# Two first-layer activations put behind the first query copies on ScalarE, and one turned tile copied by ScalarE in place of VectorE

## The chip, the core and the metric

The kernel runs on one core of one Trainium2 chip. The core has a matrix engine (TensorE, "PE" in the profile, with its weight loads listed apart as "PEld"), VectorE ("DVE"), ScalarE ("ACT"), GpSimd ("POOL") and SyncE ("SP"), which here only issues transfers. Each engine works through its own list of instructions in order, and the lists meet through semaphores. The metric is the device time of one execution in microseconds. Three runs of the kernel before gave 180.80, 180.94 and 180.96 us, so the median is 180.94 us.

## The reference

One input x of 2048 rows by 512 is layer-normalised to xn, and two branches are added to x:

```
xn = layernorm(x)
out = x + A(xn) + B(xn)

A: q, k, v = xn @ wqkv, in 32 heads of 16
   pq = q @ w_phi (per head); pk = k @ w_phi
   phi = concat(softmax(p), softmax(-p))        # 32 features per head
   kv  = sum over rows of phi_k^T v;  z = sum over rows of phi_k
   o   = (phi_q @ kv) / (phi_q . z + 1e-6);  A = o @ wo

B: act = mish(xn @ w1 + b1)                     # 512 -> 1792
   B   = act @ w2                               # 1792 -> 512
```

The attention is linear: the sums over all 2048 keys must be complete before the first query can be finished. Branch B needs no such sum, and its matrix products can be put wherever TensorE would otherwise be waiting.

## The kernel before

The 2048 rows are 16 tiles of 128 rows, in four groups of four. The order of every engine's list is the order in which the Python code issues its instructions; no scheduler changes it. The kernel keeps x, the turned xn (`xnT`), and the first layer's results (`acts`) in SBUF for the whole run.

**The head (lines 510 to 537).** The first four row tiles are normalised one by one. Each normalised tile is turned by four 128x128 transposes on TensorE into a PSUM bank (`ln_turn_pe`, line 151), and one copy takes the bank to `xnT` (line 157). The caller names the engine of this copy: tile 0 goes through ScalarE (`act`), tiles 1, 2 and 3 through VectorE (`dve`). `logits(0, i)` (line 205) multiplies turned tile i by the folded key weights `wkp` and has ScalarE copy the result to `p_sb`. On TensorE the order is: second half of the product for tile 1, transposes of tile 3 (line 532), a small transpose of the bias (line 534), products of tile 2, products of tile 3 (line 537), then the value products of the first four tiles, then six units of the first layer (`hidden(6)`, line 553), then the key products of row tile 4 (line 564).

**The key stages (lines 555 to 599).** For each group of four tiles VectorE takes maxima and minima over the 16 features (`extremes`), ScalarE the exponentials, VectorE the sums and the division (`normalise`). TensorE meanwhile does the key and value products, the accumulation of the key sums and units of the first layer. A unit (`hidden`, line 185) is one of 56: four matmuls into a bank `ph`, then one Mish activation on ScalarE (line 198), which frees the bank. Fifty-four of the 56 units are issued by line 598.

**The query stages (lines 604 to 694).** The last key stage is followed by queries in pairs of row tiles. The exponentials of a row tile go through a transposing DMA (`turn`, line 254, tile `qT`). `attend(h, i)` (line 330) handles row tile i of pair h: 32 small matmuls multiply the turned features by the masked key sums into the four banks `pnd`, then two ScalarE copies empty these banks, denominators to `ds` (line 353), numerators to `wkp` or `wv`, which are used as scratch by then (line 359). There is one `pnd` buffer, so the matmuls of an `attend` wait until both copies of the `attend` before it are done. `combine` (line 363) divides on VectorE and sends the result through a transposing DMA. `second_layer(t, f0, f1)` (line 411) adds products f0 to f1 of the 14 second-layer products of row tile t to a bank `po`. `project_out` adds the output projection to the same bank and `residual` adds x.

In this part the ordinary banks come from one pool of four, `ps`. When the first `attend` is issued they hold `po` of row tile 0, the two `ph` banks of the last two first-layer units, and `po` of row tile 1. `po` of row tile 2 therefore takes the bank of the first of the two units, and `po` of row tile 3 that of the second. The two units belong to the last group of rows; their results are read from row tile 12 on.

The lines around the second edit are 613 to 619:

```
second_layer(0)
hidden(2)
attend(0, 0)
second_layer(1, 0, 12)
attend(0, 1)
extremes(5, halves=low)
second_layer(1, 12)
```

Of the kernel before, what the change touches and what calls it, by code (L numbers as in the profile page):

```python
# [12 lines left out]
ACT = mybir.ActivationFunctionType  # L13
# [5 lines left out]
def kernel(  # L19
# [12 lines left out]
    nc = tc.nc  # L32
# [33 lines left out]
    def bank(name, dtype=FP32, pool=None):  # L66
        pool = pool or next(turns[0])
        return pool.tile([P, 512], dtype, name=name, tag="mm")

    def three_banks(name, bufs):  # L70
        stack = ExitStack()
        return stack, stack.enter_context(tc.tile_pool(name=name, bufs=bufs, space=PSUM))
# [3 lines left out]
    acts = persist.tile([P, FT, S], BF16, name="acts")  # L76
# [7 lines left out]
    b1f = wts.tile([P, FT], FP32, name="b1f")  # L84
# [66 lines left out]
    def ln_turn_pe(t, xn, i, copy):  # L151
        ptr = bank("ptr", BF16)
        for kt in range(KT):
            nc.tensor.transpose(
                ptr[:, kt * P : (kt + 1) * P], xn[:, i, kt * P : (kt + 1) * P], ident[:]
            )
        copy(xnT[:, t, :, :], ptr[:].rearrange("p (k c) -> p k c", k=KT))
# [7 lines left out]
    def project(w, t, pp=None, kts=range(KT)):  # L165

        if pp is None:
            pp = bank("pproj")[:]
        for kt in kts:
            nc.tensor.matmul(  # L170
                pp, lhsT=xnT[:, t, kt, :], rhs=w[:, kt, :],
                start=(kt == 0), stop=(kt == KT - 1),
            )
        return pp
# [7 lines left out]

    units = iter([(g, f) for g in range(NG) for f in range(FT)])

    def hidden(n, pool=None):

        for _ in range(n):
            g, f = next(units)
            ph = bank("ph", FP32, pool)
            for kt in range(KT):  # L190
                nc.tensor.matmul(  # L191
                    ph[:],
                    lhsT=w1_sb[:, kt, f * P : (f + 1) * P],
                    rhs=xnT[:, g * TPG : (g + 1) * TPG, kt, :],
                    start=(kt == 0),
                    stop=(kt == KT - 1),
                )
            nc.scalar.activation(  # L198
                acts[:, f, g * 512 : (g + 1) * 512], ph[:], ACT.Mish, bias=b1f[:, f : f + 1]
            )  # L200


    p_of, e_of, qT_of = {}, {}, {}
# [9 lines left out]
    def extremes(s, between=None, halves=(slice(0, TPG),)):  # L213

        if s not in e_of:
            e_of[s] = epool.tile([P, TPG, 2, 512], BF16, name="e")
        for q in halves:
            n = q.stop - q.start
            e = e_of[s][:, q]
            pv = p_of[s][:, q, :].rearrange("p t (c e) -> p (t c) e", e=16)  # L220
            for pl, op in enumerate((ALU.max, ALU.min)):
                if pl == 1 and between is not None:
                    between()
                src = pv
                for half in (8, 4, 2):
                    m = smx.tile([P, 128, half], BF16, name=f"m{half}", bufs=1)[:, 0 : n * 32, :]
                    nc.vector.tensor_tensor(  # L227
                        out=m, in0=src[:, :, 0:half], in1=src[:, :, half : 2 * half], op=op
                    )
                    src = m  # L230

                m = smx.tile([P, 128, 1, 2], BF16, name="m1", bufs=1)[:, 0 : n * 32]
                nc.vector.tensor_tensor(out=m[:, :, 0, :], in0=src, in1=src[:, :, ::-1], op=op)
                mb = m.rearrange("p (t c) u o -> p t c u o", t=n).to_broadcast([P, n, 32, 8, 2])
                p5 = pv.rearrange("p (t c) (e o) -> p t c e o", t=n, o=2)
                nc.vector.tensor_tensor(  # L236
                    out=e[:, :, pl, :].rearrange("p t (c e o) -> p t c e o", e=8, o=2),
                    in0=p5 if pl == 0 else mb,
                    in1=mb if pl == 0 else p5,
                    op=ALU.subtract,  # L240
                )
# [88 lines left out]
    def attend(h, i):  # L330

        if i == 0:
            nd_of[h] = (
                (wkp, wv)[h % 2][:].rearrange("p (i l) c -> p i l c", i=2),
                opool.tile([P, 2, 2, 64], FP32, name="ds"),
            )
        nm, ds = nd_of[h]
        pnd = later[0].tile([P, 4, 512], FP32, name="pnd", tag="nd")
        for pl in range(2):
            for j in range(4):  # L340
                for r in range(4):
                    at, rows = (pl * 4 + j) * 36, slice(32 * r, 32 * r + 32)
                    nc.tensor.matmul(  # L343
                        pnd[:, r, at : at + 36],
                        lhsT=qT_of[h][rows, i, pl * 4 + j, :],
                        rhs=kvm[rows, pl, j, :],
                        start=True,
                        stop=True,
                        tile_position=(32 * r, 0),
                    )  # L350
        a = pnd[:, :, 0:288].rearrange("p r (l j c) -> p l j r c", l=2, j=4)
        to = nm[:, i, :, :].rearrange("p l (j r c) -> p l j r c", j=4, r=4)
        nc.scalar.copy(  # L353
            ds[:, i].rearrange("p x (g r h) -> p g r x h", g=8, r=4),
            pnd[:, :, 0:288].rearrange("p r (g c) -> p g r c", g=8)[:, :, :, 32:36].rearrange(
                "p g r (x h) -> p g r x h", x=2
            ),
        )
        nc.scalar.copy(to, a[:, :, :, :, 0:32])
# [45 lines left out]
    def halves(t):  # L405
        return (slice(0, 256), slice(256, 512)) if t == NT - 1 else (slice(0, 512),)

    def second_layer(t, f0=0, f1=FT):
        if f0 == 0:
            po_of[t] = [  # L410
                bank("po", FP32, later[1] if c.stop == 512 and c.start else None)
                for c in halves(t)
            ]
        for po, c in zip(po_of[t], halves(t)):
            for f in range(f0, f1):
                nc.tensor.matmul(  # L416
                    po[:, c], lhsT=acts[:, f, t * P : (t + 1) * P], rhs=w2_sb[:, f, c],
                    start=(f == 0), stop=False,
                )
# [55 lines left out]
    dve, act = nc.vector.tensor_copy, nc.scalar.copy  # L475
# [10 lines left out]
    xn = lnp.tile([P, TPG, D], BF16, name="xn", tag="xn")  # L486
# [42 lines left out]
    p1 = project(wkp, 1, kts=range(0, 2))  # L529
    ln_turn_pe(2, xn, 2, dve)  # L530
    act(p_of[0][:, 1, :], project(wkp, 1, p1, kts=range(2, 4)))
    ln_turn_pe(3, xn, 3, dve)
    pb = bank("pb", BF16)
    nc.tensor.transpose(pb[:, 0:FT], b1b[:], ident[0:FT, 0:FT])
    nc.vector.tensor_copy(b1f[:], pb[:, 0:FT])
# [11 lines left out]
    xn = lnp.tile([P, TPG, D], BF16, name="xn", tag="xn")  # L547
# [3 lines left out]
    for i in range(TPG):  # L551
        value(i, act)
    hidden(6)

    for s in range(NG):
# [6 lines left out]
        if s == 0:  # L562
# [3 lines left out]
            stack, pool = three_banks("pw", 1)  # L566
# [10 lines left out]
        if ln:  # L577
            t0 = (s + 2) * TPG
            st = ln_stats(t0, TPG)
            xn = lnp.tile([P, TPG, D], BF16, name="xn", tag="xn")  # L580
# [8 lines left out]
        if s == 0:  # L589
            hidden(6)  # L590
            act(p_of[1][:, 1:4, :], wide[:])
            wide = None
            stack.close()
            pk = upper.enter_context(tc.tile_pool(name="pk", bufs=1, space=PSUM))
            pz = upper.enter_context(tc.tile_pool(name="pz", bufs=2, space=PSUM))
            hidden(6)
            turns[0] = cycle([pz, ps, ps, pz, ps, px, ps])
# [13 lines left out]
    turns[0] = cycle([ps])  # L611
    later = [after.enter_context(tc.tile_pool(name="pq", bufs=1, space=PSUM))]
    second_layer(0)
    hidden(2)
    attend(0, 0)
    second_layer(1, 0, 12)
    attend(0, 1)
    extremes(5, halves=low)
    second_layer(1, 12)
    combine(0, first)  # L620
    combine(0, last)
    extremes(5, halves=high)
# [102 lines left out]
```

## Time and profile before

The profile is of one execution of 180.87 us, 0.07 us under the median of the three runs. Its span, from the first to the last instruction, is 178.7 us; 2.1 us lie around it.

| what | value |
|---|---|
| execution profiled | 180.87 us |
| span | 178.7 us |
| TensorE clock granted | 0.999 |
| PE busy | 171.6 us, 96% of the span |
| DVE busy | 153.7 us, 86% |
| ACT busy | 124.0 us, 69% |
| ScalarE table loads for the first layer, each | 1.28 us |
| ScalarE copy of a 128x512 bank to SBUF | 0.59 us |
| VectorE copy of a turned 128x512 tile | 0.41 to 0.42 us |

All times inside the profile are counted from the start of the span. Busy shares say little on what a given edit is worth; the chain of waits and the timeline of the stage that is edited say more. Ends of matmuls are modelled in the records, so short gaps on PE are best read from the starts of successive matmuls.

### The profile page before, as it was taken

How to read it: one execution, taken by the hardware profiler on the slowest of the kernel's cores; microseconds unless marked ns; L12 is line 12 of the kernel's file. 1: busy time of each engine (PE TensorE's matmuls, PEld its weight loads, DVE VectorE, ACT ScalarE, POOL GpSimd, SP SyncE). 2: the span in 40 equal slices, each digit the busy share in tenths (PEclk: the TensorE clock that was granted, in tenths of full speed). 3: DMA queues.
4: the chain of work that ended last, by engine and by line, in shares of the span. 5: the costliest groups of instructions: out<-in, count | busy, mean ns of one | idle time of the engine just before them, and what ended most of it. 6: DMA issues, size and time to landing. Idle time of an engine off the chain costs nothing.

```text
span 178.7 us, 4338 instructions
## 1 busy us (share of the span) xinstructions
PE 171.6 (96%) x1806; PEld 81.7 (46%) x1806; DVE 153.7 (86%) x305; ACT 124.0 (69%) x166; POOL 28.5 (16%) x40
## 2 busy tenths in 40 slices
PE   6799999999999999999999989999999999999992
PEld 2454444454444545544454444444444444444561
DVE  1989799999999989998999969798789979789853
ACT  3657999997998799969994988388223854552200
POOL 5203029900799300000000000000000000000000
PEclk9999999999999999999999999999999999999999
DMA  5997794330023600000000883919983096394843
GB/s 143 292 417 271 137 366 144 59 64 0 4 53 64 121 0 0 4 4 0 0 4 0 159 80 71 110 31 146 201 126 90 0 150 118 88 122 120 67 115 115
DMA packets 44559, 18.12 MB, mean 101 GB/s; under 512 B 36988, under 2 KB 44028, under 8 KB 44540
## 3 DMA queue, kind: packets, MB, share of 16 engines
q1 hardware_dynamic: 43712, 17.57, 46.8%
q10 hardware_dynamic: 828, 0.28, 0.6%
q8 instruction: 14, 0.23, 0.6%
q14 instruction: 5, 0.04, 0.1%
HBM read 6.84 MB, written 2.10 MB: 50 GB/s over the span
## 4 chain that ended last, share of the span: by engine, by line
DVE 46%; PE 42%; ACT 5%; DMA 4%; issue 2%; DVEq 0%; ACTq 0%
PE po L416 21%; DVE s L268 10%; PE pproj L170 8%; PE po L425 6%; DVE m L227 6%; DVE e L281 6%; DVE e L236 6%; DVE r L276 4%; PE ph L191 3%; DVE stats L130 3%; ACT e L249 2%; PE pnd L343 2%; DMA qT<-e 2%; DMA x_sb<-in_A_x_dram 2%; DVE r L277 2%
## 5 line engine op out<-in xcount | busy, mean ns | idle before, releaser
L416 PE MATMUL po<-w_sb,acts 128*128 128x512 bf16 (+1 forms) x238 | 51.0, 367 | 0.2 <-DVE x_sb L433 0.2
L191 PE MATMUL ph<-xnT,w_sb 128*128 128x512 bf16 x224 | 49.5, 379 | 0.0
L249 ACT ACTIVATE e<-e 128x2048 bf16<-128x2048 bf16 (+1 forms) x17 | 30.2, 1808 | 7.8 <-DVE e L236 7.8
L198 ACT ACTIVATE acts<-ph,b1f 128x512 bf16<-128x512 f32 x56 | 34.4, 706 | 1.5 <-PE ph L191 1.4
L191 PEld LDWEIGHTS <-w_sb 128*128 128x128 bf16 x224 | 21.9, 98 | 26.4 <-issue 0.3
L416 PEld LDWEIGHTS <-acts 128*128 128x128 bf16 x238 | 22.2, 98 | 22.7 <-issue 0.2
L170 PEld LDWEIGHTS <-xnT 128*128 128x128 bf16 x192 | 18.3, 98 | 21.8 <-issue 1.1
L268 DVE TENSOR_REDUCE s<-e 128x128 f32<-128x2048 bf16 x8 | 18.2, 2273 | 1.6 <-ACT e L249 1.6
L353 ACT COPY ds<-pnd 128x128 f32<-128x128 f32 x16 | 4.4, 275 | 17.7 <-PE pnd L343 15.5
L142 POOL TENSOR_SCALAR xn<-x_sb,mv,rstd 128x512 bf16<-128x512 bf16 x8 | 16.6, 2084 | 0.2
L433 DVE TENSOR_TENSOR x_sb<-po,x_sb 128x512 bf16<-128x512 f32 (+1 forms) x17 | 10.9, 658 | 6.6 <-PE po L425 6.5
L425 PE MATMUL po<-wqk,ob 128*128 128x512 bf16 (+1 forms) x68 | 15.1, 367 | 0.0
L170 PE MATMUL pproj<-wv,xnT 128*128 128x512 bf16 x64 | 15.0, 379 | 0.0
L227 DVE TENSOR_TENSOR m<-m 128x256 bf16<-128x256 bf16 (+2 forms) x44 | 13.4, 304 | 1.5
L170 PE MATMUL pproj<-wqk,xnT 128*128 128x512 bf16 x64 | 14.5, 379 | 0.0
L211 ACT CAST p_sb<-pproj 128x512 bf16<-128x512 f32 x20 | 10.8, 587 | 3.8 <-PE pproj L170 2.3
L170 PE MATMUL pproj<-wkp,xnT 128*128 128x512 bf16 x52 | 12.6, 379 | 0.1
L281 DVE TENSOR_TENSOR e<-e,r 128x2048 bf16<-128x2048 bf16 x8 | 10.7, 1337 | 0.3
L227 DVE TENSOR_TENSOR m<-p_sb 128x1024 bf16<-128x1024 bf16 (+1 forms) x18 | 10.2, 565 | 0.0
L425 PEld LDWEIGHTS <-ob 128*128 128x128 bf16 x68 | 6.4, 97 | 7.0 <-DMA ob<-ob 0.4
L236 DVE TENSOR_TENSOR e<-p_sb,m 128x2048 bf16<-128x2048 bf16 (+1 forms) x9 | 8.9, 989 | 0.3
L236 DVE TENSOR_TENSOR e<-m,p_sb 128x2048 bf16<-128x2048 bf16 (+1 forms) x9 | 8.9, 989 | 0.3
(73 smaller groups left out, 173.7 us busy)
## 6 DMA issues: line engine op xcount, KB each, us to landing
w_sb<-in_B_w_dram SPq DMA_DIRECT2D x2, 1792.0 KB, 8.4
out_dram<-x_sb SPq DMA_DIRECT2D x15, 128.0 KB, 1.9
x_sb<-in_A_x_dram SPq DMA_DIRECT2D x1, 1024.0 KB, 11.0
x_sb<-in_A_x_dram SPq DMA_DIRECT2D x1, 512.0 KB, 4.1
wv<-in_A_wqkv_dram SPq DMA_DIRECT2D x1, 512.0 KB, 4.8
wqk<-in_A_wo_dram SPq DMA_DIRECT2D x1, 512.0 KB
x_sb<-in_A_x_dram SPq DMA_DIRECT2D x1, 256.0 KB, 3.1
x_sb<-in_A_x_dram ACTq DMA_DIRECT2D x1, 256.0 KB, 3.5
```

What stands on the lines that cost most here:

```text
L142: engine.tensor_scalar(out=xn[:, at + i, :], in0=x_sb[:, t0 + i, :], scalar1=mv[:, i, 0:1], scalar2=rstd[:, i : i + 1], op0=ALU.subtract, ...
L170: nc.tensor.matmul(pp, lhsT=xnT[:, t, kt, :], rhs=w[:, kt, :], start=(kt == 0), stop=(kt == KT - 1),)
L191: nc.tensor.matmul(ph[:], lhsT=w1_sb[:, kt, f * P : (f + 1) * P], rhs=xnT[:, g * TPG : (g + 1) * TPG, kt, :], start=(kt == 0), stop=(kt == ...
L198: nc.scalar.activation(acts[:, f, g * 512 : (g + 1) * 512], ph[:], ACT.Mish, bias=b1f[:, f : f + 1])
L227: nc.vector.tensor_tensor(out=m, in0=src[:, :, 0:half], in1=src[:, :, half : 2 * half], op=op)
L236: nc.vector.tensor_tensor(out=e[:, :, pl, :].rearrange("p t (c e o) -> p t c e o", e=8, o=2), in0=p5 if pl == 0 else mb, in1=mb if pl == 0 ...
L249: nc.scalar.activation(v, v, ACT.Exp)
L268: nc.vector.reduce_sum(t[:], v.rearrange("p t l (c e) -> p (t l c) e", e=16), axis=AX.X)
L281: nc.vector.tensor_tensor(out=vv, in0=vv, in1=r2[:, :, None, :].to_broadcast([P, 128, 8, 2]), op=ALU.mult)
L416: nc.tensor.matmul(po[:, c], lhsT=acts[:, f, t * P : (t + 1) * P], rhs=w2_sb[:, f, c], start=(f == 0), stop=False,)
L425: nc.tensor.matmul(po[:, c], lhsT=oT_of[h][:, t % 2 * 4 + j, :], rhs=wo_sb[:, j, c], start=False, stop=(j == 3),)
L433: nc.vector.tensor_tensor(out=y, in0=po[:, c], in1=y, op=ALU.add)
```

## The change

There are two edits.

The copy of the fourth turned tile (tile 3) goes from VectorE to ScalarE. On ScalarE it stands between the copies of the logits of tile 1 and tile 2. VectorE's list is one instruction shorter, ScalarE's one longer.

The last two units of the first layer keep their matmuls where they were, but their two Mish activations are held back and issued after `attend(0, 0)`. On ScalarE the two copies of `attend(0, 0)` then come first, followed by the table load for Mish, the two activations, and the copies of `attend(0, 1)`. Two of the second-layer products of row tile 1 move from ahead of `attend(0, 1)` to behind it, so there are ten ahead and four behind. The number of table loads stays the same, since copies ask for none.

```diff
-    def hidden(n, pool=None):
+    def hidden(n, pool=None, late=None):
...
-            nc.scalar.activation(
-                acts[:, f, g * 512 : (g + 1) * 512], ph[:], ACT.Mish, bias=b1f[:, f : f + 1]
-            )
+            if late is None:
+                activate(g, f, ph)
+            else:
+                late.append((g, f, ph))
+
+    def activate(g, f, ph):
+        nc.scalar.activation(
+            acts[:, f, g * 512 : (g + 1) * 512], ph[:], ACT.Mish, bias=b1f[:, f : f + 1]
+        )
...
-    ln_turn_pe(3, xn, 3, dve)
+    ln_turn_pe(3, xn, 3, act)
...
     second_layer(0)
-    hidden(2)
+    late = []
+    hidden(2, late=late)
     attend(0, 0)
-    second_layer(1, 0, 12)
+    for unit in late:
+        activate(*unit)
+    second_layer(1, 0, 10)
     attend(0, 1)
     extremes(5, halves=low)
-    second_layer(1, 12)
+    second_layer(1, 10)
```

## The prediction

> **What bounds the kernel now.** I read the page first, then the chain of waits in order of time, then the timelines of the two places that the change edits, 9.5 to 13.8 us and 100 to 113 us. The page gives two engines that are nearly full, and a chain that is shared between them:
>
> ```profile
> span 178.7 us, 4338 instructions
> PE 171.6 (96%) x1806; PEld 81.7 (46%) x1806; DVE 153.7 (86%) x305; ACT 124.0 (69%) x166; POOL 28.5 (16%) x40
> DVE 46%; PE 42%; ACT 5%; DMA 4%; issue 2%; DVEq 0%; ACTq 0%
> ```
>
> The chain in order of time (start, length, what) tells which engine holds which stretch:
>
> ```profile
> 10.76 5.29 PE pproj L170 x24
> 16.04 5.18 PE ph L191 x24
> 21.22 0.88 PE pproj L170 x4
> 22.12 0.69 DVE p_sb L564
> ...
> 98.00 3.19 DMA qT<-e
> 101.24 0.46 PE pnd L343 x32
> ...
> 104.89 0.38 PE pnd L343 x32
> 105.27 3.56 PE po L416 x16
> ```
>
> From about 8 to 22 us PE holds the path, without a gap; from 22 to 98 VectorE does; from 101 to 155 PE again; VectorE from 155 to 165 and PE to the end. The reader should see that the first edit lies in a PE stretch although it lightens VectorE, and that the second lies where PE takes over. There PE has one real gap, and the timeline names its cause:
>
> ```profile
> 101.21 1.28 ACT L198 ACT_TABLE_LOAD   x1
> 102.51 1.27 ACT L198 ACTIVATE acts<-ph,b1f 128x512 bf16<-128x512 f32 x2
> 103.66 0.27 ACT L353 COPY ds<-pnd 128x128 f32<-128x128 f32 x1
> 103.81 1.03 ACT L359 CAST wkp<-pnd 128x1024 bf16<-128x1024 f32 x1
> 104.89 0.38 PE L343 MATMUL pnd<-kvm,qT 32*128 32x36 bf16 x32 [0.59 <-ACT wkp L359]
> 105.37 0.28 ACT L353 COPY ds<-pnd 128x128 f32<-128x128 f32 x1 [0.53 <-PE pnd L343]
> ```
>
> The first query's matmuls are done at about 101.7, but ScalarE first loads a table and runs two activations, so the copies that free `pnd` end at 104.84 and the second query starts at 104.89. For the head:
>
> ```profile
> 10.46 0.59 ACT L531 CAST p_sb<-pproj 128x512 bf16<-128x512 f32 x1 [0.50 <-PE pproj L170]
> 10.68 0.42 DVE L157 COPY xnT<-ptr 128x512 bf16<-128x512 bf16 x1 [0.23 <-PE ptr L154]
> 11.76 0.59 ACT L211 CAST p_sb<-pproj 128x512 bf16<-128x512 f32 x1 [0.72 <-PE pproj L170]
> 22.12 0.69 DVE L564 CAST p_sb<-pproj 128x512 bf16<-128x512 f32 x1 [1.06 <-PE pproj L170]
> ```
>
> **First edit, the fourth turned tile.** VectorE loses one copy of 0.42 us. The bias copy of 0.16 us behind it still has to wait for its own transpose, whose record ends at 10.76, so VectorE is ahead by about 0.25 us, not 0.42. That is worth nothing: at 22.12 VectorE stands idle for 1.06 us for a PE product, and PE's stretch up to there is gapless, so it waits 1.3 us instead. What covers it is PE's 11 us of products from 10.76 on.
>
> ScalarE gains a copy of 0.59 us (tile 0's copy, same shape, is 0.59 at 6.64). It stands in a hole: 0.72 us of idle time before the cast at 11.76. Two casts back to back take 1.07 us from 7.17 on, so a second starts 0.48 us after the first; the new copy would start at 10.46 + 0.48 = 10.94 and end at 11.53. The cast at 11.76 is not delayed. But PE needs this tile: products of tile 2 run at one per 0.216 us from 10.69, so tile 3's first is due at 11.56, and its weight load stood at 11.35. From an engine's end to PE's start the rows show 0.05 us (ScalarE ends 104.84, PE starts 104.89), so the weights can be loaded from 11.58 on. The stall is at least 0.02 us, if the matmul may follow its load at once, as at 10.69 where both are recorded together; at most 0.22, if the copy waits for the full end of the cast at 11.05 (end 11.64, plus 0.05) and a whole weight load of 0.10 is exposed. I take 0.07, nearer the overlapping start, since the rows at 7.17 show ScalarE starting early. PE has no gap between here and 22.1, nor VectorE from there to 98 (it only waits for exponentials that it fed itself), so this stall goes to the end in full: +0.07.
>
> **Second edit, the order around the first query.** TensorE's matmuls are the same in number. From one `attend` to the next the rows give 3.44 us with 14 products between (108.76 to 112.20) and 3.87 with 16 (104.89 to 108.76): 0.215 per product and 0.43 fixed. Without a wait the second query would have started at 101.24 + 0.43 + 12 x 0.215 = 104.25; it started at 104.89. The wait is 0.64 us (the timeline says 0.59, from a modelled end).
>
> In the changed order ScalarE is free at 101.20 and takes the first query's copies when its matmuls are done. At the second query the copy starts 0.48 us after the matmuls (105.37 against 104.89), so here at 101.72, or 0.04 later for the wait on two semaphores in its queue: 101.76. The numerators' copy follows 0.17 later and frees `pnd` at 102.95. TensorE comes to the second query after ten products, at 101.24 + 0.43 + 2.15 = 103.82, 0.87 us later than that. Its turned features landed at 102.61 by the trace's landing events, so they don't hold it. Two products fewer ahead means two more behind, and the third query starts at 103.82 + 0.43 + 18 x 0.215 = 108.12 instead of 108.76: -0.64. If only the record's gap of 0.59 counts, -0.59.
>
> What is queued behind the copies: table load 102.96 to 104.24, activations 104.25 to 105.52, the second query's denominators at about 105.39. Before, these stood at 105.37. So ScalarE is no later for anything behind, its idle 0.53 us has only moved ahead of the first copies; its exponential stays at 107.87. The activations themselves are late by 1.75 us. Their results are not read for 40 us, but their banks are: `po` of row tile 2 takes the first one's bank, a wait that the changed program carries on that first matmul. PE comes there at 103.82 + 0.31 + 4 x 0.215 = 104.99; the first activation ends 0.69 after its start, at 104.94, plus 0.05 is 104.99. That is a dead heat: between 0 and, if every step on ScalarE slips a little, 0.12. I take 0.02.
>
> One rule speaks against this order. The rows show a table load beginning within 0.02 us of the end of the work before it (101.21 after 101.19; 106.57 after 106.56) and the next activation 0.01 to 0.02 after it. The Trainium skill, "ScalarE: Activation LUTs", section "What ACT_TABLE_LOAD costs", adds a drain of about 1.38 us to each load of 1.283; by it the first activation would end near 106.3 and the sum would be slower by some 0.8 us instead. The trace agrees on the load's 1.28 and shows no drain in any of its other loads, so the sum goes by the rows.
>
> VectorE can combine the first row tile from 102.93 instead of 103.97, the second when its denominators come at 105.66, with the numerators at 106.56 on time: about 0.6 us earlier than before, and SP issues the two transposing DMAs behind it earlier (106.42 and 108.74 before). No queue is passed: SP's order is unchanged. PE needs their result at about 111.9; it landed at 111.36 even before.
>
> Does the 0.64 last? The next claim on ScalarE's own pace is `pnd` for the fourth query: ScalarE is busy with exponentials until 109.78, its copies end at 110.85, PE now comes at 111.56: 0.7 us to spare. By 112.68 ScalarE waits 1.83 us for PE, by 113.58 VectorE waits 1.04 us, so from there everything is paced by PE and moves with it, the VectorE stretch from 155 included, whose start waits on a PE product (0.90 us idle at 155.03).
>
> **Sum.** -0.64 + 0.02 + 0.07 = -0.55 us against the profiled execution of 180.87 us, which is 180.32. That execution is 0.07 under the median of 180.94; a median of the changed kernel may lie as much above the sum.
>
> **Rivals.**
> 1. Forecast: about 180.3, faster by 0.3%. Chance 0.73, own range 180.1 to 180.5.
> 2. The gain shrinks below about what a measurement of this kernel can tell from no change (0.2%, 0.36 us): tile 3's stall at its upper 0.22 and the bank wait at 0.12, with the gain at 0.59, gives -0.25, so 180.6. For it: both waits are close races. Against: each would have to come out at its worst end. Chance 0.12.
> 3. The gain is hidden: PE runs 0.64 earlier into another wait that doesn't move, ScalarE's copies for the fourth query or the DMA for the projection. Then only the head's stall is left: 180.87 + 0.07 = 180.9. Against: 0.7 and over 1 us to spare. Chance 0.06.
> 4. Slower: the first `ph` bank comes late. If the changed place of the table load costs ScalarE as much again as one load, 1.28 us, row tile 2's first product waits 1.28 us at 104.99, and -0.64 + 1.28 + 0.07 + 0.02 gives 181.6. It decides from 0.6 us of lateness on. Against: no load in the rows costs more than 1.3 us with its edges. The drain that the Trainium skill states in the section named above would do this. Chance 0.09, with other ways to be slower in it.
>
> The predicted time is that of case 1. The range 180.05 to 180.75 holds cases 1 and 2 with a run's scatter (0.16 us over the three runs). Faster by over 0.2%: 0.73; within 0.2%: 0.18; slower: 0.09.
>
> **What would show it.** Right: on ScalarE denominators at about 101.8, the table load at about 103; no wait of PE on `wkp` before the second query, which starts near 103.9; the third query near 108.2; PE's idle time down by about 0.5 us; VectorE's wait at 22 us grown to 1.3. Wrong: a wait of PE on `acts` before row tile 2, a weight load of tile 3 waiting on ScalarE for more than 0.2 us, or the fourth query waiting on `wv`.

## The result, and the profile after

The changed kernel takes 180.30 us (median of eight runs) against 180.88 us for the kernel before in the same session. One of the eight, the profiled one, ran at a granted TensorE clock of 0.76, took 225.76 us and is left out of everything that follows. The other seven lie between 180.09 and 180.57, with a mean of 180.28 and a median of 180.19. Their ratio to the kernel before is 0.9967, with a 95% interval of 0.9956 to 0.9978: faster by 0.60 us, between 0.40 and 0.80. The forecast was 180.32 us. All lines of "after" below are of a second session of the same kernel, whose profiled execution took 180.09 us with the clock at 1.000. There the ratio is 0.9949, interval 0.9936 to 0.9961.

In the changed kernel's file, lines behind `hidden` have moved down by six: 343 is 349, 353 is 359, 359 is 365, 416 is 422, 425 is 431, 433 is 439 and 564 is 570.

The page after, first lines and the chain by engine:

```profile
span 178.0 us, 4338 instructions
PE 171.9 (97%) x1806; PEld 81.6 (46%) x1806; DVE 153.4 (86%) x304; ACT 124.5 (70%) x167; POOL 28.5 (16%) x40
...
PE 87%; DVE 8%; DMA 2%; issue 0%; DVEq 0%
```

VectorE has one instruction less, ScalarE one more, TensorE is at 97%. The chain is now followed back along TensorE for nearly the whole span. That does not mean that VectorE has become fast: in this execution TensorE reached the first query just as its data did (the data landed at 101.29 us, the matmuls start at 101.33), so at that point the inferred chain could turn either way. In the profile of the second edit alone, where the first query starts at the same 101.33, the page gives VectorE 45% and TensorE 43%.

The place of the second edit, in the timeline after (ScalarE, then TensorE):

```profile
100.72 0.56 ACT L217 CAST p_sb<-pproj 128x512 bf16<-128x512 f32 x1
101.86 0.27 ACT L359 COPY ds<-pnd 128x128 f32<-128x128 f32 x1 [0.58 <-ACT p_sb L217]
102.02 1.02 ACT L365 CAST wkp<-pnd 128x1024 bf16<-128x1024 f32 x1
103.06 1.28 ACT L204 ACT_TABLE_LOAD   x1
104.35 1.26 ACT L204 ACTIVATE acts<-ph,b1f 128x512 bf16<-128x512 f32 x2
105.51 0.27 ACT L359 COPY ds<-pnd 128x128 f32<-128x128 f32 x1
```

```profile
101.33 0.37 PE L349 MATMUL pnd<-kvm,qT 32*128 32x36 bf16 x32
101.64 2.33 PE L422 MATMUL po<-w_sb,acts 128*128 128x512 bf16 x10
103.90 0.37 PE L349 MATMUL pnd<-kvm,qT 32*128 32x36 bf16 x32
104.21 4.06 PE L422 MATMUL po<-w_sb,acts 128*128 128x512 bf16 x18
108.20 0.37 PE L349 MATMUL pnd<-kvm,qT 32*128 32x36 bf16 x32
```

The copies of the first query come first and free `pnd` at 103.04; TensorE comes at 103.90 and does not wait. The wait of 0.59 us on `wkp` is gone. From the first query to the third it now takes 6.87 us (101.33 to 108.20); before it was 7.52 (101.24 to 108.76), as this line of the kernel before shows with the ones of the prediction:

```profile
108.76 0.37 PE L343 MATMUL pnd<-kvm,qT 32*128 32x36 bf16 x32
```

That is 0.65 us gained, and the eighteen products run on across the bank that the late activation frees. The single starts show how close that was: the first product of row tile 2 starts at 105.090, 0.050 us after the first activation ends (105.040) and 0.222 us after the product before it, where the usual distance is 0.216. So TensorE lost 0.006 us there.

The head (ScalarE, TensorE's weight loads, VectorE):

```profile
10.54 0.58 ACT L537 CAST p_sb<-pproj 128x512 bf16<-128x512 f32 x1 [0.50 <-PE pproj L170]
11.02 0.59 ACT L157 COPY xnT<-ptr 128x512 bf16<-128x512 bf16 x1
...
11.66 0.98 PEld L170 LDWEIGHTS <-xnT 128*128 128x128 bf16 x6 [0.35 <-ACT xnT L157]
...
22.24 0.69 DVE L570 CAST p_sb<-pproj 128x512 bf16<-128x512 f32 x1 [1.32 <-PE pproj L170]
```

TensorE's weight loads pause for 0.35 us before tile 3's. Counted from the first product of tile 2, tile 3's first weight load comes 0.90 us later, before 0.66, so it is 0.24 us late. In the kernel before it stood 0.214 us, a whole matmul, ahead of the product that uses it, and that covers most of the delay: from the first product of tile 2 to the first value product the starts are 1.773 us apart, before 1.737. The stall is 0.04 us. VectorE waits 1.32 us for the key product instead of 1.06.

0.65 less 0.04 is 0.61, yet the span is 0.75 us shorter, although this execution's first rows of x landed about 0.1 us later (VectorE's first statistics start at 4.05, before at 3.95) and its first query started 0.10 us later. At the third query it is 0.56 us ahead of the kernel before, at SyncE's last instruction named DRAIN 0.57, at the end of the span 0.75. So about 0.2 us came from somewhere that the sum did not have, and it came at the very end. The experiments were aimed at that, and at the two close races.

### The profile page after: what moved, and what is told of

It reads as the page before. It is cut to its first block, busy times and chain, and to the rows that moved or that the text cites. A ratio compares the mean times of both kernels' runs of the same rounds, so it can differ in the third digit from the quotient of the medians.

```text
span 223.7 us, 4338 instructions
## 1 busy us (share of the span) xinstructions
PE 219.0 (98%) x1806; PEld 92.5 (41%) x1806; DVE 154.7 (69%) x304; ACT 129.0 (58%) x167; POOL 28.7 (13%) x40
## 4 chain that ended last, share of the span: by engine, by line
PE 95%; DMA 3%; SPq 0%; DVE 0%; issue 0%
PE po L422 29%; PE ph L191 28%; PE pproj L170 23%; PE po L431 8%; DMA wT<-in_A_wqkv_dram 3%; PE pnd L349 2%; PE pkv L302 2%; PE pwide L170 2%; PE pfold L112 1%; PE ptr L154 0%; SPq L449 0%; DVE x_sb L439 0%; PE pb L540 0%
## 5 line engine op out<-in xcount | busy, mean ns | idle before, releaser
L422 PE MATMUL po<-w_sb,acts 128*128 128x512 bf16 (+1 forms) x238 | 65.4, 442 | 0.0
L191 PE MATMUL ph<-xnT,w_sb 128*128 128x512 bf16 x224 | 64.7, 462 | 0.0
L204 ACT ACTIVATE acts<-ph,b1f 128x512 bf16<-128x512 f32 x56 | 37.5, 687 | 16.5 <-PE ph L191 16.4
L191 PEld LDWEIGHTS <-w_sb 128*128 128x128 bf16 x224 | 25.1, 112 | 38.0 <-issue 38.0
L422 PEld LDWEIGHTS <-acts 128*128 128x128 bf16 x238 | 25.4, 112 | 31.9 <-issue 29.3
L431 PE MATMUL po<-wqk,ob 128*128 128x512 bf16 (+1 forms) x68 | 19.3, 443 | 0.0
L170 PE MATMUL pproj<-wv,xnT 128*128 128x512 bf16 x64 | 19.2, 458 | 0.0
L170 PE MATMUL pproj<-wqk,xnT 128*128 128x512 bf16 x64 | 18.8, 462 | 0.0
L170 PE MATMUL pproj<-wkp,xnT 128*128 128x512 bf16 x52 | 15.8, 459 | 0.0
L178 DVE CAST vext<-pproj 128x512 bf16<-128x512 f32 x6 | 4.1, 691 | 14.3 <-PE pproj L170 14.3
```

The lines of the kernel that those rows point to most:

```text
L170: nc.tensor.matmul(pp, lhsT=xnT[:, t, kt, :], rhs=w[:, kt, :], start=(kt == 0), stop=(kt == KT - 1),)
L191: nc.tensor.matmul(ph[:], lhsT=w1_sb[:, kt, f * P : (f + 1) * P], rhs=xnT[:, g * TPG : (g + 1) * TPG, kt, :], start=(kt == 0), stop=(kt == ...
L204: nc.scalar.activation(acts[:, f, g * 512 : (g + 1) * 512], ph[:], ACT.Mish, bias=b1f[:, f : f + 1])
L422: nc.tensor.matmul(po[:, c], lhsT=acts[:, f, t * P : (t + 1) * P], rhs=w2_sb[:, f, c], start=(f == 0), stop=False,)
L431: nc.tensor.matmul(po[:, c], lhsT=oT_of[h][:, t % 2 * 4 + j, :], rhs=wo_sb[:, j, c], start=False, stop=(j == 3),)
```

## The experiments

Every time below is compared with runs of the kernel before in the same session; ratios have 95% intervals, and the microseconds are the ratio's difference from 1 times the median of before.

### Both edits again, and each alone

First the changed kernel itself, from which the lines above come.

> Both edits, nothing else, for an undisturbed profile. Theory (the gap at the second query closed, a small stall in the head, a dead heat at row tile 2's bank): -0.55 us against the kernel before; denominators' copy at about 101.8, table load about 103.0, second query about 103.9, third about 108.2; weight load of tile 3 waits on ScalarE 0.02 to 0.2 us. Rival (the bank comes late): PE waits on acts before row tile 2's first product by 0.1 us or more. Rival (the gain is hidden behind a later wait): third query 0.6 us earlier, but PE's start on the row tiles after 113 us no earlier than before.

Measured: 0.9949 (0.9936 to 0.9961), 180.11 us against 181.07. The events came within 0.1 us of the forecast's marks (101.86, 103.06, 103.90, 108.20). There is no wait on `acts` in its list of waits, and the starts above put the bank's share at 0.006 us, so the bank is not late by anything that counts. The shift is not hidden either: the first matmul behind the fourth query's projection, at 114.32 us before, starts at 113.76, and from the fifth query to SyncE's last drain it takes 60.22 us in the changed kernel and 60.23 before.

Then the first edit alone (the edit is against the changed kernel, as the next one is):

```diff
-    hidden(2, late=late)
+    hidden(2)
...
-    second_layer(1, 0, 10)
+    second_layer(1, 0, 12)
...
-    second_layer(1, 10)
+    second_layer(1, 12)
```

> The first edit alone: tile 3 copied by ScalarE, the order around the first query as before. Theory: +0.07 us against the kernel before (0.02 to 0.22), PE's weight load of tile 3 waits on ScalarE, VectorE's wait before the key product's copy grows from 1.06 to about 1.3 us. Rival (the lighter VectorE counts): faster by up to 0.25 us, the 0.25 us by which VectorE gets ahead.

Measured: 0.9989 (0.9980 to 0.9999), faster by 0.20 us (0.02 to 0.36), not slower by 0.07. The theory's sign is wrong for this edit taken alone, though each event in the head came as it said. Its list of waits has the 1.3 us of VectorE, the 0.4 us of the weight load, and still the 0.6 us before the second query:

```profile
DVE p_sb L570 <- PE pproj L170: 1.3, 1, 1.3
...
PE pnd L349 <- ACT wkp L365: 0.6, 1, 0.6
...
PEld L170 <- ACT xnT L157: 0.4, 1, 0.4
```

The rival, that the lighter VectorE counts, would need VectorE's 0.25 us to reach the end; but VectorE gives it all back in the wait before its copy of the key product. So neither explained the gain. In this profile the first query comes 0.34 us later than in the kernel before (most of it from the start-up that the last section describes), SyncE's last drain 0.33 us later, but the end of the span only 0.14: again it is behind that drain that something was gained.

The second edit alone:

```diff
-    ln_turn_pe(3, xn, 3, act)
+    ln_turn_pe(3, xn, 3, dve)
```

> The second edit alone: the two activations behind the first query's copies, ten products ahead of the second query, tile 3 copied by VectorE as before. Theory: -0.62 us against the kernel before, 0.07 us better than both edits together. Rival (the head's edit is the one that helps): no better than before by more than 0.3 us.

Measured: 0.9962 (0.9948 to 0.9975), 0.69 us faster (0.45 to 0.94). That is the forecast's term for this edit. But it is not better than both edits together; in medians it is 0.27 us worse (180.38 against 180.11).

### Is the moved split needed?

> The activations held back as in the change, but twelve products ahead of the second query as before, tile 3 copied by VectorE. Theory: the second query starts at about 104.25 with pnd free since 102.95, no wait either way, and the third query at 108.12 as with ten: -0.62 us, the same as with the split moved. Rival (the split is needed for the gain): 0.3 us or more worse than with ten ahead.

```diff
-    second_layer(1, 0, 10)
+    second_layer(1, 0, 12)
...
-    second_layer(1, 10)
+    second_layer(1, 12)
```

(against the second edit alone). Measured: 0.9959 (0.9947 to 0.9972), 0.74 us faster than before. From the first query to the third it took 6.87 us here as well (101.46 to 108.33 by the starts of their matmuls). Holding the activations back does it all; the split from twelve to ten is free in either position once `pnd` is early.

The opposite, the split moved and the activations left where they were (again against the second edit alone):

```diff
-    hidden(2, late=late)
+    hidden(2)
```

> Ten products ahead of the second query instead of twelve, with the two activations ahead of the first query's copies as before. Theory: the second query still waits for the copies at about 104.9, and two products now lie behind it instead of in front, so the wait grows from 0.64 to 1.07 us and the time by 0.43. Rival (the split itself brings a gain): not slower than before.

Measured: 1.0026 (1.0016 to 1.0036), slower by 0.47 us (0.29 to 0.65); the 0.43 expected lies inside. With `pnd` late, a product moved behind the wait is a product's time lost; that fits the time, but the longer wait itself was read from no trace.

### How close is the race for the bank?

To the second edit alone a second table load was added in front of the held-back activations. It computes nothing that is used.

```diff
+    nc.scalar.activation(root[:], eps[:], ACT.Sqrt)
     for unit in late:
         activate(*unit)
```

> The second edit alone with one more table load ahead of the held-back activations (a square root of a 128x1 constant into an unused one forces a change of table and back; it computes nothing). Theory (the first activation and TensorE's return to its bank meet within some 0.1 us): PE now waits about 1.3 to 1.5 us on the activation before row tile 2's first product, and the time rises by about that much against the second edit alone, to 0.7 to 0.9 us slower than before; the third query follows at about 109.6. Rival (there is room at this bank): less than 0.7 us of it is seen in the time.

Measured: 1.0035 (1.0022 to 1.0048), 0.63 us slower than the kernel before, against 0.69 faster without the extra load: 1.32 us between them. ScalarE and TensorE in its timeline:

```profile
102.97 1.28 ACT L623 ACT_TABLE_LOAD   x1
104.27 0.20 ACT L623 ACTIVATE root<-eps 128x1 f32<-128x1 f32 x1
104.48 1.28 ACT L204 ACT_TABLE_LOAD   x1
105.77 1.26 ACT L204 ACTIVATE acts<-ph,b1f 128x512 bf16<-128x512 f32 x2
```

```profile
104.13 1.04 PE L422 MATMUL po<-w_sb,acts 128*128 128x512 bf16 x4
106.51 3.18 PE L422 MATMUL po<-w_sb,acts 128*128 128x512 bf16 x14 [1.35 <-ACT acts L204]
109.62 0.37 PE L349 MATMUL pnd<-kvm,qT 32*128 32x36 bf16 x32
```

From the start of the first table load to the first activation it takes 2.80 us (102.97 to 105.77); in the changed kernel it is 1.29 (103.06 to 104.35). The activation is thus 1.51 us later. From the first query to the third it takes 8.37 us instead of 6.87: 1.50 us of lateness, 1.50 us of stall, nothing absorbed. The bank has no room, and the rival that it has is out. Between the two times there are 0.18 us less than the stall. That is the size of the next finding, and this kernel's ScalarE list is longer too, but each of the two times is uncertain by more than 0.2 us, so it is no test of it.

These rows also settle what the table load costs here: 1.28 us and at most 0.02 us on either side of it, with two loads around an activation of 0.20 us. The drain of about 1.38 us that the Trainium skill, "ScalarE: Activation LUTs", section "What ACT_TABLE_LOAD costs", adds to each load did not appear in them.

### Where the first edit gains: the close of the program

With and without the first edit, the traces differ in their last microsecond. Behind the last store, all engines meet in a closing barrier; each engine's records there have a last instruction named DRAIN, called its last drain here. SyncE's last drain came 2.09 to 2.10 us after the last store was issued in every one of the nine kernels below, but ScalarE's did not keep to that: in some kernels it came with SyncE's, in some 0.27 to 0.29 us after it. The page has one visible trace of this, the second instruction queue. Before and after:

```profile
q14 instruction: 5, 0.04, 0.1%
```

```profile
q14 instruction: 6, 0.05, 0.1%
```

The sixth packet is a block of 8 KB of instructions. (In the kernel before, a sixth block is fetched too, but after the end of the span, where the page does not count it.) The first edit makes ScalarE's list one instruction longer. Two kernels test whether that alone does it, with tile 3 on VectorE as before and one idle copy added to ScalarE in the hole of the head: on the kernel before, and on the second edit alone.

```diff
     ln_turn_pe(3, xn, 3, dve)
+    act(root[:], eps[:])
```

> The kernel before with one more instruction on ScalarE: a copy of a 128x1 constant into an unused one, in ScalarE's idle 0.7 us of the head. It computes nothing. Theory (what the first edit gains lies in the closing barrier, where a ScalarE list of this length is fetched to its end in time): from SyncE's last drain to the end of the span 0.45 us instead of 0.63, six packets on the second instruction queue instead of five, about 0.18 us faster than the kernel before, with tile 3 still copied by VectorE. Rival (the first edit gains because VectorE is lighter): no faster than the kernel before, 0.63 us at the close.

> The second edit alone plus that same idle copy on ScalarE; tile 3 copied by VectorE. Theory: 0.18 us faster than the second edit alone through the close, and without the head's stall of 0.04 us, so level with both edits together or 0.04 us better: 0.8 us faster than the kernel before. Rival: like the second edit alone, 0.64 us faster than before.

As a control the same idle copy was put on VectorE:

```diff
     ln_turn_pe(3, xn, 3, dve)
+    nc.vector.tensor_copy(root[:], eps[:])
```

> The kernel before with the idle copy of a 128x1 constant put on VectorE instead of ScalarE; it computes nothing. A control for the close. Theory (it is the length of ScalarE's list that matters): 0.63 us from SyncE's last drain to the end, as in the kernel before, and the last fetch of instructions only after 178 us. Rival (any shift of the program's instructions changes the close): 0.45 us.

From the records of the barrier and of the instruction queue in each trace (us from the start of the span):

```
kernel                          ScalarE list   SP's last  ACT's last  to the end of  last 8 KB
                                vs. before     drain      drain       the span       fetch
before                               0         178.11     178.40      0.63           179.2
second edit alone                    0         177.59     177.88      0.63           178.5
late activations, split of 12        0         177.67     177.94      0.63           178.6
idle copy on VectorE                 0         178.14     178.43      0.63           179.1
idle copy on ScalarE                +1         178.32     178.33      0.45           167.8
first edit alone                    +1         178.44     178.44      0.45           168.2
both edits                          +1         177.55     177.55      0.45           167.3
second edit, idle copy on ScalarE   +1         177.90     177.91      0.46           167.7
second edit, table loaded twice     +2         178.97     178.97      0.45           167.5
```

The column of list lengths counts the instructions added, table loads among them; the last column is the start of the fetch. There is one profiled execution of each kernel. Every kernel with the old length closes in 0.63 us, every kernel with a longer list in 0.45 to 0.46, for the three kinds of instruction that were added (a copy of a tile, an idle copy, a table load with its activation); lengthening VectorE's list does nothing. In the longer ones the last 8 KB block is fetched at 167 to 168 us, about 10 us ahead of the barrier. In the others it is fetched 0.3 to 0.5 us after the end of the span, so ScalarE's late drain, which starts 0.65 to 0.80 us before that fetch, cannot have waited for this block to arrive. Late drain and late fetch go together in every trace; what delays the drain is not shown.

The row of the second edit with the idle copy has a late SyncE drain for another reason. From the fifth query to that drain it takes 60.76 us there, and 60.22 to 60.27 in the other eight kernels. In that execution, which took 180.46 us where the median is 180.09, TensorE waited 0.77 us at 164 us for a DMA into `ob`, against 0.29 in the second edit alone.

In time: the idle copy alone measured 0.9998 (0.9986 to 1.0010), which can't tell 0.18 us (0.1%) from nothing, since that kernel's twelve runs lie between 180.61 and 181.52. Its expected gain was thus not seen in the time, only at the close. The second edit with the idle copy measured 0.9948 (0.9933 to 0.9963), level with both edits (0.9949), and its median is 180.09 against 180.11, though in another session. The 0.27 us by which both edits beat the second alone is more than the 0.18 less 0.04 that the traces account for; with five runs each, the rest may be scatter. The single execution with the idle copy on VectorE took 180.87 us beside 181.02 for the kernel before, which is no difference by the scatter seen here.

So the change's first edit is worth its place only by accident: the copy of tile 3 by ScalarE costs 0.04 us, and the other additions to ScalarE's list, which do nothing useful, brought the same 0.18 at the close. The two terms give -0.14 for this edit alone, inside the interval of the 0.20 us (0.02 to 0.36) that it measured.

## Why the prediction was right, and where it was not

**The time, the sign and the second edit** came as forecast. The term of -0.64 us measured -0.65 in the trace, from the distance between the first query and the third, and -0.69 (-0.45 to -0.94) in the time of that edit alone. The reasoning that ScalarE is no later for anything behind held to within 0.05 us: the second query's denominators start at 105.51, before at 105.37, in an execution that ran 0.10 us later at the first query. The shift went through to the end, because ScalarE and VectorE both wait for TensorE at 112 to 114 us (1.15 and 0.97 us in the changed kernel).

**The dead heat at the bank** was sized at 0.02 us (0 to 0.12) and measured 0.006. The doubled table load shows that the race is as tight as computed: 1.50 us of lateness gave 1.50 us of stall.

**The table switch**, the rival that would have ended slower, was priced right in its mechanism. A switch that costs 1.5 us more does make the kernel slower than before, by 0.63 us. In the changed kernel itself it did not happen: the load at 103.06 took the 1.28 us of the rows, and the activation began 0.01 us behind it.

**The stall in the head** was taken as 0.07 us and measured 0.04. The copy started 0.48 us after the cast before it and the weights were loaded 0.05 us after its end, both as worked out; the exposed weight load cost almost nothing, so the lower bound (0.02) was nearer than the value taken.

**The step that failed** is the sum over the first edit. "+0.07" was its whole price, and the rest of the edit, ScalarE's list longer by one instruction, was given none. By the trace it brought -0.18 us at the close. With it the sum would have been -0.65 + 0.04 - 0.18 = -0.79, against -0.75 between the two profiled spans. The fuller sum lies inside both intervals, 0.60 us (0.40 to 0.80) in the first session and 0.92 (0.71 to 1.16) in the second; the forecast's 0.55 lies only in the first. That the forecast of 180.32 came within 0.04 us of the first session's 180.28 is therefore partly luck.

**The rivals** of a gain that shrinks or is hidden are out: third query, the products behind the fourth query's projection and SyncE's last drain all move by 0.56 or 0.57 us.

## What to carry to other kernels

Work that nobody reads soon, and above all a table load, should stand behind the copies that free a single-buffered bank, not in front of them; before moving it, look up who takes the buffer that the delayed work holds, since here that bank came due within a few hundredths of a microsecond. Where two experiments differ by a tenth of a percent, compare the close of the program and the lengths of the engines' lists before giving the credit to the edit. Price a wait between engines by the starts of successive matmuls, not by modelled ends: 0.64 from the starts was right, 0.59 from the gap was low.

## What was not expected of the hardware

The closing barrier took 0.63 or 0.45 us, depending on the length of ScalarE's list and on nothing else that was varied, and a block of 8 KB was fetched about 11 us earlier where it took 0.45.

The kernel's warm-up on TensorE, eleven matmuls in the first microseconds, does not always take the same time. Two executions, the changed kernel's and that of the first edit alone:

```profile
1.42 3.98 PE L487 MATMUL warm<-ident 128*128 128x512 bf16 x11 [1.42 <-POOL eps L462]
6.31 0.40 PE L154 MATMUL ptr<-ident,xn 128*128 128x128 bf16 x4 [0.91 <-DVE xn L511]
```

```profile
1.42 4.88 PE L487 MATMUL warm<-ident 128*128 128x512 bf16 x11 [1.42 <-POOL eps L462]
6.37 0.61 PE L154 MATMUL ptr<-ident,xn 128*128 128x128 bf16 x4
```

The cause is in the traces' record of the granted TensorE clock, which shows full clock from a certain moment on. Up to that moment the warm-up's matmuls start about 0.43 us apart, behind it about 0.21. It came at 4.14 to 4.36 us in four of the nine kernels' profiled executions, the changed kernel's (4.36) among them, and at 4.99, 5.48, 5.93, 6.90 (the first edit alone) and 7.42 in the others. Where it came after the warm-up's last matmul had started (5.93 and later), the warm-up took 4.76 to 4.88 us, the first key product started at 8.12 to 8.16 us and the first query at 101.45 to 101.58; in the other six it took 3.87 to 4.53, and the two started at 7.75 to 7.92 and 101.16 to 101.33. That is 0.1 to 0.4 us at the first query, as much as half of what the change brings, whatever the kernel. It is part of the scatter between runs, but it does not explain all of it: the kernel with one idle copy on ScalarE has runs in two groups, 180.61 to 180.86 and 181.08 to 181.52 us, and its profiled execution, with full clock last of all, took 180.86 and belongs to the faster group.
